# Multi-resolution attention with a mixture-of-experts stage: the loads are issued by GpSimd instead of ScalarE

## The chip, the cores and the metric

The program runs on one core of a Trainium2 chip. The metric is device time in microseconds of one execution, as the median of several runs. The engines are written as in the profile: PE (TensorE), DVE (VectorE), ACT (ScalarE), POOL (GpSimd) and SP (SyncE). Each of them takes its own instructions in one fixed order. A name with a q, as ACTq, is the engine's sequencer, which waits on semaphores and issues DMAs.

## The reference

For each of 8 batches, 8 heads, 576 tokens and a head dimension of 64, two attentions are added and then 128 tokens per batch go through a small feed-forward block:

```
q_d, k_d, v_d = means of q, k, v over groups of 4 tokens
out_up    = repeat(softmax(q_d k_d^T / 8) v_d, 4 times along the tokens)
out_local = softmax(q k^T / 8 where |i - j| < 4, else -1e9) v
x = (out_up + out_local) laid out as [batch, 576, 512]
scores = x . w_gate
for each batch: top = the 128 tokens of the highest score
    out[top] = x[top] + sigmoid(scores[top]) * (relu(x[top] @ w1) @ w2)
```

The feed-forward block is called MoE below.

## The kernel before

**Stages of one batch b.** `load_qk` brings q and k of a batch into the tile `T` in two DMAs (half the head pairs each, two runs of 4.6 KB per partition), `load_vw` brings windows of v into `vw` in three DMAs, and the first step of `pool_v` brings v in groups of four tokens into `vraw` in one DMA. `pool_qk` (VectorE) sums groups of four tokens of `T` into `dT`, and the rest of `pool_v` (GpSimd, lines 207 to 213) does the same for `vraw` into `vd` and `vr`, three sums and one product. `coarse` computes the coarse attention in two units; its second unit ends with the tile `ods` (L319), which SyncE stores to a DRAM buffer `up_d` with four copies of each row. `load_up` reads that back as `x` (SyncE). `local` computes the banded attention in three units of two, two and one tiles of 116 tokens; each tile ends with `t` on VectorE (L451). `sums` lets GpSimd add `x` and `t` (L469), five sums to a batch, and SyncE stores each group to the output. `route` ranks the tokens; VectorE writes the row numbers `idx` (L528), and GpSimd gathers the 128 rows back from the output into `xe` with an indirect DMA (L536). TensorE transposes them (`px`, L544), `moe` runs the two matrix products with the weights `w1` and `w2` (held as two f16 parts, made from the f32 staging tiles `stg` by ScalarE and VectorE in `load_weights`), and GpSimd scatters the rows back with a second indirect DMA (L587).

**Order of the work.** The stages are generators, and the table `PLACE` with the list `events` says at which point of the batch's period each step is traced. A load of batch b+1 is traced in the period of batch b: the `vraw` load at 0.217 of it, the three `vw` loads at 0.675, 0.925 and 1.175, the two `T` loads at -0.1 and 0.0 before the period in which they are pooled; the eight weight loads at 0.07 to 1.09 of the first period. `route` and `moe` of batch b run in the periods of b+1 and b+2. A planner then orders each engine's instructions by a simulated time line. What goes through the class `InOrder` (line 48 on, recorded in the profile under L55) is pinned: it is issued no earlier than the instruction that was traced just before it on the same engine. GpSimd's sums, products and indirect DMAs are not pinned and the planner may move them.

**What a DMA waits for.** The DMAs that ScalarE and SyncE issue share eight semaphores in turn. The next DMA on a semaphore is issued only once the one before on it has landed, whichever engine issued that.

**Buffers.** `T` and `vraw` have two buffers, `stg` four, `vw` one for each of its three parts.

**Lines.** `load_constants` 113 to 132, `load_weights` 142 to 165, `load_qk` 169 to 176, `load_vw` 192 to 198, `pool_v` 202 to 217, `sums` L466 to 478, `route` L481 to 552, `moe` from L555.

Of the kernel before, what the change touches and what calls it, by code (L numbers as in the profile page):

```python
# [21 lines left out]
P = 128  # L22
# [36 lines left out]
def tile_multires_attention_moe(ctx: ExitStack, tc: tile.TileContext, qk, vw, vp, cs, w_gate, w1, w2, outs):  # L59


    nc = tc.nc
    B, _, _, HP, S = qk.shape
    pool = nc.gpsimd
    sp, aq, vq = (InOrder(tc, e) for e in (nc.sync, nc.scalar, nc.vector))
    D = P // 2
    H = 2 * HP
    DM = H * D
# [22 lines left out]
    cst = cpool.tile([P, sum(CONST.values())], F32, name="cst")  # L91
    at = dict(zip(CONST, np.cumsum([0, *CONST.values()]).tolist()))

    def const(n):
        return cst[:, at[n] : at[n] + CONST[n]]

    wg = cpool.tile([P, DM], F32, name="wg")
# [15 lines left out]
    def load_constants():  # L113
        n = at["first"]
        sp.dma_start(out=cst[:, :n], in_=cs[:, :n])
        for t in (*qzbuf, *pzbuf, first):
            pool.memset(t, 0.0)
        pool.memset(ones, 1.0)
        nc.vector.tensor_copy(identb, ident)
        nc.vector.tensor_copy(mask.rearrange("p e t k -> p (e t k)"), const("mask"))  # L120
        for t in vals:
            nc.vector.tensor_copy(t[:, :, 0], const("tok"))
        nc.vector.tensor_copy(pen, const("pen"))
        nc.vector.tensor_copy(off, const("off"))
        yield
        aq.dma_start(out=wg, in_=w_gate.unsqueeze(0).broadcast_to([P, DM]))
        aq.dma_start(
            out=wgr, in_=w_gate.rearrange("(h d) -> h d", d=D).unsqueeze(1).broadcast_to([H, SR, D])
        )
        aq.dma_start(out=cst[:, n:], in_=cs[:, n:])  # L130
        pool.tensor_copy(first[:, :P], const("first"))
        yield

# [8 lines left out]
    def load_weights():  # L142
        pend = []

        def convert(sv, h_, l_):
            aq.activation(h_, sv, AF.Copy, scale=WS)
            vq.scalar_tensor_tensor(out=l_, in0=sv, scalar=WS, in1=h_, op0=ALU.mult, op1=ALU.subtract)

        for src, hi, lo, n in ((w1, w1h, w1l, DF), (w2, w2h, w2l, DM)):
            for i in range(4):  # L150
                cc = hi.shape[1] // 4
                stg = ld.tile([P, 4 * 256], F32, tag="stg", name="stg", bufs=4)
                sv = stg.rearrange("p (c f) -> p c f", f=n)
                aq.dma_start(
                    out=sv, in_=src[i * cc * P : (i + 1) * cc * P, :].rearrange("(c p) f -> p c f", p=P)
                )
                cs_ = slice(i * cc, (i + 1) * cc)
                pend.append((sv, hi[:, cs_, :], lo[:, cs_, :]))
                if len(pend) == 4:
                    convert(*pend.pop(0))  # L160
                yield
        while pend:
            convert(*pend.pop(0))
            yield
# [4 lines left out]
    def load_qk(b):  # L169
        qkT[b] = wk.tile([P, 2, HP, S], F32, tag="T", name=f"T{b}")  # L170
        hh = HP // 2
        for u in range(2):
            aq.dma_start(
                out=qkT[b][:, :, hh * u : hh * (u + 1)], in_=qk[b][:, :, hh * u : hh * (u + 1)]
            )
            yield
# [15 lines left out]
    def load_vw(b):  # L192
        vwin[b] = []
        for i, tiles in enumerate(TU):
            t = wk.tile([P, 2 * len(tiles), HP, D1], F32, tag=f"vw{i}", name=f"vw{b}_{i}", bufs=1)
            aq.dma_start(out=t, in_=vw[b][:, 2 * tiles[0] : 2 * tiles[-1] + 2])
            vwin[b].append(t)
            yield

# [1 line left out]

    def pool_v(b):
        raw = ld.tile([P, FACTOR, DM + D], F32, tag="vraw", name="vraw", bufs=2)
        aq.dma_start(out=raw, in_=vp[b])
        yield
        vd = vds[b] = wk.tile([P, DM + D], F32, tag="vd", name=f"vd{b}")
        pool.tensor_tensor(out=vd, in0=raw[:, 0], in1=raw[:, 1], op=ALU.add)  # L207
        for r in range(2, FACTOR):
            pool.tensor_tensor(out=vd, in0=vd, in1=raw[:, r], op=ALU.add)
        yield  # L210

        vrs[b] = wk.tile([P, H, D], F32, tag="vr", name=f"vr{b}", bufs=1)
        pool.tensor_tensor(
            out=vrs[b], in0=vd[:, DM:].unsqueeze(1).broadcast_to([P, H, D]),
            in1=bk.unsqueeze(2).broadcast_to([P, H, D]), op=ALU.mult,
        )
        yield
# [413 lines left out]
    nu = len(WU)  # L631
    mains = []
    consts = load_constants()
    next(consts)
    lqk = [put(lambda b=b: load_qk(b), 2, *when("QK", b, b - 1)) for b in range(B)]
    weights = None
    for b in range(B):
        pq = put(lambda b=b: pool_qk(b), 5, *when("PL", b, b - 1), lqk[b])
        pv = put(lambda b=b: pool_v(b), 3, *when("VP", b, b - 1))
        lv = put(lambda b=b: load_vw(b), 3, *when("VW", b, b - 1))  # L640
        if weights is None:
            put(lambda: consts, 1, *when("CS", 0, -1))
            weights = put(load_weights, 11, *when("WT", 0, 0))
        for i in range(nu):
            need = (pq, pv) if i < 2 else ()
            g = put(lambda b=b, i=i: unit(b, i), 0, 0, 0, *need)
            e0, e1 = ends[i], ends[i + 1]
            for ph in range(3):
                events.append((b + e0 + PH[ph] * (e1 - e0), len(events), g, ph == 2))
            mains.append(g)  # L650
        xl = put(lambda b=b: load_up(b), 1, *when("XL", b, b))
        xsums[b] = put(lambda b=b: sums(b), 3, *when("XS", b, b), xl)
        rt = put(lambda b=b: route(b, scs[b]), 15, *when("RT", b, b + 1), *mains[-nu:])
        put(lambda b=b: moes[b], 16, *when("MO", b, b + 1), weights, rt)
# [81 lines left out]
```

## Time and profile before

| | |
|---|---|
| median of 3 runs | 380.62 us (380.48 to 385.15) |
| profiled execution | 377.89 us, its span 376.1 us |
| busy PE / DVE / ACT / POOL | 287.4 / 248.9 / 143.8 / 127.4 us |
| share of the span | 76% / 66% / 38% / 34% |
| DMA moved | 78.25 MB, mean 208 GB/s |
| mean granted TensorE clock | 0.841 |

Times in the rows are microseconds from the start of the span. A row of the time line has the start, the length, the engine, the line of the code, the operation, the tile written, the tile read, and in brackets how long the engine had been idle and what ended that. A busy engine is one that executes; waiting and issuing by its sequencer is not counted, except for GpSimd's DMAs, which count as GpSimd's own work.

### The profile page before, as it was taken

How to read it: one execution, taken by the hardware profiler on the slowest of the kernel's cores; microseconds unless marked ns; L12 is line 12 of the kernel's file. 1: busy time of each engine (PE TensorE's matmuls, PEld its weight loads, DVE VectorE, ACT ScalarE, POOL GpSimd, SP SyncE). 2: the span in 40 equal slices, each digit the busy share in tenths (PEclk: the TensorE clock that was granted, in tenths of full speed). 3: DMA queues.
4: the chain of work that ended last, by engine and by line, in shares of the span. 5: the costliest groups of instructions: out<-in, count | busy, mean ns of one | idle time of the engine just before them, and what ended most of it. 6: DMA issues, size and time to landing. Idle time of an engine off the chain costs nothing.

```text
span 376.1 us, 10940 instructions
## 1 busy us (share of the span) xinstructions
PE 287.4 (76%) x4624; PEld 224.8 (60%) x4624; DVE 248.9 (66%) x534; ACT 143.8 (38%) x401; POOL 127.4 (34%) x99
## 2 busy tenths in 40 slices
PE   0680677717799999949996789919997799984984
PEld 0470546606687688638854677619865588673571
DVE  2595867995489777966776658855778667575030
ACT  0541357621445364513623264413624255424010
POOL 1505530471306630753045410733146410351111
PEclk9996556865699999957999599966999589998598
DMA  8897999782686969774777397765687343733100
GB/s 309 294 408 245 281 324 359 256 219 56 218 293 215 251 229 337 202 204 137 262 271 199 106 292 288 190 200 149 240 281 223 86 132 116 200 95 72 28 30 28
DMA packets 32832, 78.25 MB, mean 208 GB/s; under 512 B 7824, under 2 KB 7824, under 8 KB 31760
## 3 DMA queue, kind: packets, MB, share of 16 engines
q10 hardware_dynamic: 11048, 43.72, 33.5%
q1 hardware_dynamic: 20456, 29.65, 28.1%
q0 software_dynamic: 1280, 4.20, 3.5%
q8 instruction: 36, 0.59, 0.6%
q14 instruction: 12, 0.10, 0.1%
HBM read 56.58 MB, written 20.97 MB: 206 GB/s over the span
## 4 chain that ended last, share of the span: by engine, by line
PE 35%; DMA 30%; DVE 14%; issue 10%; ACT 7%; SPq 2%; POOL 1%; ACTq 1%; POOLq 0%; DVEq 0%
DMA up_d<-ods 11%; DMA x<-up_d 7%; DMA xe<-out_dram,idx 6%; ACT ed L262 4%; DMA out_dram<-xe,idx 3%; PE od L296 3%; PE ph L564 3%; PE ol L441 3%; PE ph L567 3%; PE sd L237 2%; PE ph L568 2%; PE pspl L429 2%; DMA T<-in_qk_dram 2%; SPq L55 2%; PE sl L407 2%
## 5 line engine op out<-in xcount | busy, mean ns | idle before, releaser
L469 POOL TENSOR_TENSOR x<-x,t 128x512 f32<-128x512 f32 x40 | 64.5, 1618 | 71.7 <-DVE t L451 55.4
L567 PE MATMUL ph<-xel,w1h 128*128 128x128 f16 x256 | 49.2, 230 | 1.6 <-DVE xel L548 1.6
L564 PE MATMUL ph<-xeh,w1h 128*128 128x128 f16 x256 | 49.7, 231 | 0.8 <-ACT xeh L547 0.7
L207 POOL TENSOR_TENSOR vd<-vraw 128x576 f32<-128x576 f32 x8 | 12.1, 1512 | 111.4 <-DMA vraw<-in_vp_dram 97.3
L568 PE MATMUL ph<-xeh,w1l 128*128 128x128 f16 x256 | 49.1, 230 | 0.0
L441 PE MATMUL ol<-vw,pt 64*64 64x65 f32 x1280 | 33.7, 255 | 19.9 <-DVE den L450 10.1
L55 DVE TENSOR_REDUCE dT<-T 128x288 f32<-128x1152 f32 x32 | 42.8, 1343 | 4.0 <-DMA T<-in_qk_dram 4.0
L441 PEld LDWEIGHTS ol<-vw,pt 64*64 64x64 f32 x1280 | 28.3, 163 | 25.3 <-ACT qz L189 10.4
L429 PE MATMUL pspl<-cst,ex 128*128 128x128 f32 x160 | 28.0, 315 | 11.5 <-ACT ex L423 11.5
L423 ACT ACTIVATE ex<-ex 128x1024 f32<-128x1024 f32 (+1 forms) x24 | 21.9, 913 | 33.3 <-DVE ex L419 17.5
L407 PE MATMUL sl<-T 64*58 64x64 f32 (+1 forms) x1280 | 33.6, 230 | 0.0
L456 DVE SCALAR_TENSOR_TENSOR jk<-t,wg 128x512 f32<-128x512 f32 x40 | 30.4, 763 | 1.0
L451 DVE TENSOR_TENSOR t<-ol,den 128x512 f32<-128x512 f32 x40 | 27.6, 692 | 4.0 <-DVE den L450 0.5
L407 PEld LDWEIGHTS sl<-T 64*58 64x58 f32 (+1 forms) x1280 | 28.2, 138 | 2.7 <-issue 0.8
L431 ACT COPY pt<-pspl 128x512 f32<-128x512 f32 x40 | 22.3, 582 | 19.1 <-PE pspl L429 18.9
L564 PEld LDWEIGHTS <-w1h 128*128 128x128 f16 x256 | 26.9, 105 | 3.1 <-issue 1.9
L429 PEld LDWEIGHTS pspl<-cst,ex 128*128 128x128 f32 x160 | 20.5, 161 | 13.7 <-ACT ex L423 12.0
L568 PEld LDWEIGHTS <-w1l 128*128 128x128 f16 x256 | 26.7, 104 | 2.2 <-issue 1.8
L567 PEld LDWEIGHTS <-w1h 128*128 128x128 f16 x256 | 26.8, 105 | 0.4
L262 ACT ACTIVATE ed<-sd,mxd 128x144 f32<-128x144 f32 x64 | 25.9, 524 | 0.5
L503 DVE SCALAR_TENSOR_TENSOR beat<-srow,scp,first 128x640 bf16<-128x640 f32 (+4 forms) x40 | 25.6, 673 | 0.0
L416 DVE TENSOR_REDUCE mx<-sl 128x16 f32<-128x1024 f32 (+1 forms) x24 | 24.8, 1033 | 1.1 <-PE sl L407 1.1
(132 smaller groups left out, 589.2 us busy)
## 6 DMA issues: line engine op xcount, KB each, us to landing
T<-in_qk_dram ACTq DMA_DIRECT2D x16, 1152.0 KB
vraw<-in_vp_dram ACTq DMA_DIRECT2D x8, 1152.0 KB
vw<-in_vw_dram ACTq DMA_DIRECT2D x16, 520.0 KB
up_d<-ods SPq DMA_DIRECT2D x8, 1024.0 KB
x<-up_d SPq DMA_DIRECT2D x32, 256.0 KB
out_dram<-x SPq DMA_DIRECT2D x32, 192.0 KB
stg<-in_moe_w_dram ACTq DMA_DIRECT2D x8, 512.0 KB
vw<-in_vw_dram ACTq DMA_DIRECT2D x8, 260.0 KB
```

Of the source, the lines that this page charges most:

```text
L55: return lambda *a, **k: self.tc.keep_in_program_order(f(*a, **k))
L262: nc.scalar.activation(ed[:, :, h] if h < H else er, s[:, a, SD * i : SD * (i + 1)], AF.Exp, bias=mx[:, c : c + 1], scale=pscale, accum_ou ...
L407: nc.tensor.matmul(s[64 * e : 64 * e + qn, a, c : c + KW], lhsT=T[64 * a : 64 * a + 64, 0, hp, q0s[blk] : q0s[blk] + qn], rhs=T[64 * a : 6 ...
L429: nc.tensor.transpose(ps[:, hp, :], ex[:, HP * i + hp, :], ident)
L441: nc.tensor.matmul(o[64 * e : 64 * e + 64, a, D1 * hp : D1 * (hp + 1)], lhsT=pt[64 * a : 64 * a + 64, hp, 64 * e : 64 * e + 64], rhs=vl[64 ...
L451: nc.vector.tensor_tensor(out=t.rearrange("p (g a d) -> p a g d", a=2, d=D), in0=ov[:, :, :, 0:D], in1=den.unsqueeze(3).broadcast_to([P, 2 ...
L456: nc.vector.scalar_tensor_tensor(out=jk, in0=t, scalar=1.0, in1=wg, op0=ALU.mult, op1=ALU.mult, accum_out=sc[:, j : j + 1],)
L469: pool.tensor_tensor(out=x[:, i], in0=x[:, i], in1=ts[b][j], op=ALU.add)
L503: nc.vector.scalar_tensor_tensor(out=beat[:, : NT - j].rearrange("p j u -> p (j u)"), in0=sr[:, P * j :], scalar=scp[:, j : j + 1], in1=fi ...
L564: nc.tensor.matmul(ph[:, i, :], lhsT=w1h[:, c, fs], rhs=xeh[:, c, :], start=c == 0, stop=False)
L567: nc.tensor.matmul(ph[:, i, :], lhsT=w1h[:, c, fs], rhs=xel[:, c, :], start=False, stop=False)
L568: nc.tensor.matmul(ph[:, i, :], lhsT=w1l[:, c, fs], rhs=xeh[:, c, :], start=False, stop=c == NC - 1)
```

## The change

All 59 loads from the inputs (three constants' loads, eight of weights, sixteen of `T`, twenty-four of `vw`, eight of `vraw`) are issued by GpSimd through `InOrder` instead of by ScalarE. The stores, the loads of `x` and the first load of constants stay with SyncE; the conversions of the weights stay pinned on ScalarE and VectorE.

```diff
-    sp, aq, vq = (InOrder(tc, e) for e in (nc.sync, nc.scalar, nc.vector))
+    sp, aq, vq, lq = (InOrder(tc, e) for e in (nc.sync, nc.scalar, nc.vector, nc.gpsimd))
...
-        aq.dma_start(out=wg, in_=w_gate.unsqueeze(0).broadcast_to([P, DM]))
-        aq.dma_start(
+        lq.dma_start(out=wg, in_=w_gate.unsqueeze(0).broadcast_to([P, DM]))
+        lq.dma_start(
             out=wgr, in_=w_gate.rearrange("(h d) -> h d", d=D).unsqueeze(1).broadcast_to([H, SR, D])
         )
-        aq.dma_start(out=cst[:, n:], in_=cs[:, n:])
+        lq.dma_start(out=cst[:, n:], in_=cs[:, n:])
         pool.tensor_copy(first[:, :P], const("first"))
...
                 sv = stg.rearrange("p (c f) -> p c f", f=n)
-                aq.dma_start(
+                lq.dma_start(
...
         for u in range(2):
-            aq.dma_start(
+            lq.dma_start(
                 out=qkT[b][:, :, hh * u : hh * (u + 1)], in_=qk[b][:, :, hh * u : hh * (u + 1)]
...
-            aq.dma_start(out=t, in_=vw[b][:, 2 * tiles[0] : 2 * tiles[-1] + 2])
+            lq.dma_start(out=t, in_=vw[b][:, 2 * tiles[0] : 2 * tiles[-1] + 2])
...
-        aq.dma_start(out=raw, in_=vp[b])
+        lq.dma_start(out=raw, in_=vp[b])
```

## Rows read from the trace of the kernel before

**Rows 1.** The page: busy time of the engines, and DMA share in 40 slices.
```profile
PE 287.4 (76%) x4624; PEld 224.8 (60%) x4624; DVE 248.9 (66%) x534; ACT 143.8 (38%) x401; POOL 127.4 (34%) x99
...
DMA  8897999782686969774777397765687343733100
```

**Rows 2.** Stretches: length, busy us (instructions) of each engine, clock, DMA share, GB/s.
```profile
24.00:67.00 43.00, 25.31 (x439) 20.23 (x427) 31.97 (x59) 18.44 (x45) 13.66 (x9) 0.64 0.95 317
...
148.00:190.00 42.00, 35.40 (x561) 28.08 (x551) 29.78 (x65) 17.03 (x49) 15.80 (x11) 0.84 0.72 220
```

**Rows 3.** The page: the chain that ended last, shares by engine.
```profile
PE 35%; DMA 30%; DVE 14%; issue 10%; ACT 7%; SPq 2%; POOL 1%; ACTq 1%; POOLq 0%; DVEq 0%
```

**Rows 4.** Time line of PE, 0 to 112 us: start, length, work, idle before.
```profile
36.93 1.97 PE L429 MATMUL pspl<-cst,ex 128*128 128x128 f32 x8 [8.49 <-ACT ex L423]
...
48.99 1.12 PE L429 MATMUL pspl<-cst,ex 128*128 128x128 f32 x4 [2.99 <-ACT ex L423]
...
86.41 1.09 PE L544 MATMUL px<-cst,xe 128*128 128x128 f32 x4 [10.14 <-DMA xe<-out_dram,idx]
```

**Rows 5.** Time line of ACT and its queue, 0 to 190 us.
```profile
0.74 1.32 ACTq L55 DMA_DIRECT2D T<-in_qk_dram  x2
...
14.68 0.57 ACTq L55 DMA_DIRECT2D T<-in_qk_dram  x1
...
20.51 0.39 ACTq L55 DMA_DIRECT2D vraw<-in_vp_dram  x1
...
35.44 0.34 ACTq L55 DMA_DIRECT2D stg<-in_moe_w_dram  x1
35.82 1.06 ACT L423 ACTIVATE ex<-ex 128x1024 f32<-128x1024 f32 x1 [9.33 <-DMA up_d<-ods]
...
47.36 1.06 ACT L55 ACTIVATE w1h<-stg 128x1024 f16<-128x1024 f32 x1 [5.94 <-DMA x<-up_d]
...
62.90 0.37 ACTq L55 DMA_DIRECT2D vraw<-in_vp_dram  x1
...
158.14 0.34 ACTq L55 DMA_DIRECT2D vw<-in_vw_dram  x1
```

**Rows 6.** Time line of POOL, the whole span.
```profile
2.10 0.09 POOL L118 MEMSET ones<- 128x1 bf16 x1
12.67 1.40 POOL L207 TENSOR_TENSOR vd<-vraw 128x576 f32<-128x576 f32 x1 [10.48 <-DMA vraw<-in_vp_dram]
...
17.23 1.04 POOL L213 TENSOR_TENSOR vr<-vd,cst 128x512 f32<-128x512 f32 x1
31.77 1.88 POOL L207 TENSOR_TENSOR vd<-vraw 128x576 f32<-128x576 f32 x1 [13.50 <-DMA vraw<-in_vp_dram]
...
42.21 6.34 POOL L469 TENSOR_TENSOR x<-x,t 128x512 f32<-128x512 f32 x4 [4.49 <-DMA x<-up_d]
...
70.87 1.40 POOL L207 TENSOR_TENSOR vd<-vraw 128x576 f32<-128x576 f32 x1 [15.77 <-DMA vraw<-in_vp_dram]
...
77.45 1.95 POOL L536 DMA_INDIRECT xe<-out_dram,idx  x1 [0.17 <-DMA x<-up_d]
...
159.43 2.95 POOL L469 TENSOR_TENSOR x<-x,t 128x512 f32<-128x512 f32 x2 [1.64 <-DMA x<-up_d]
162.53 0.98 POOL L536 DMA_INDIRECT xe<-out_dram,idx  x1 [0.15 <-issue]
```

**Rows 7.** Time line of DVE, 0 to 112 us.
```profile
74.81 0.15 DVE L528 CAST idx<-pi 128x1 int32<-128x1 f32 x1
```

**Rows 8.** Groups of POOL: count, then busy us, mean ns, idle before, and releasers.
```profile
L536 POOL DMA_INDIRECT xe<-out_dram,idx x8 | 9.1, 1136 | 35.5 <-DVE den L449 19.4 <-DVE idx L528 12.0 <-DMA out_dram<-x 3.5
...
L587 POOL DMA_INDIRECT out_dram<-xe,idx x8 | 8.1, 1006 | 24.2 <-DVE xe L586 24.1 <-issue 0.2
```

**Rows 9.** The page: DMA issues, count and KB each.
```profile
T<-in_qk_dram ACTq DMA_DIRECT2D x16, 1152.0 KB
...
vw<-in_vw_dram ACTq DMA_DIRECT2D x16, 520.0 KB
```

## The prediction

> **What bounds the kernel now.** I read the page first: PE is busy 76% of the span, DVE 66%, ACT only 38% and POOL 34%, and the DMA engines are nearly full in the first seven slices and less so after [rows 1]. So a mean tells nothing, and I cut the span into stretches. From 24 to 67 us, DMA is the full resource (0.95 busy, 317 GB/s) while PE works 25 of 43 us at a clock of 0.64; from 148 to 190, one period of the steady part, PE works 35 of 42 us and DMA is at 0.72 [rows 2]. The start is a matter of transfers and their order, the steady part of PE and of what PE waits for. The chain that ended last says the same: PE 35%, DMA 30%, and the issuing queue that the change empties, ACTq, 1% [rows 3].
>
> Then I asked what PE waits for. Two waits early on, 8.49 and 2.99 us, end with ACT, and one of 10.14 us, at 86.41, ends with the landing of the first gather [rows 4]. ACT itself was held in the first case: its `ex` at 35.82 came 9.33 us late, after the landing of an `up_d` store, because a weight load stood ahead of it in the queue and waited for a semaphore that the store of SyncE still held; the conversion at 47.36 came 5.94 us late behind a load of `x` in the same way [rows 5]. These two stalls are what the change takes away for certain.
>
> The gather at 77.45 is the other thing to see [rows 6]. Its row numbers were there at 74.96 [rows 7], but in POOL's queue it stands behind the four operations of `vd` and `vr`, which started at 70.87 when `vraw` had landed after 15.77 us of idling [rows 6]. That `vraw` load was issued at 62.90 [rows 5]. So the first long wait of PE hangs, over POOL's fixed order, on the moment when the third `vraw` load is issued. The same order holds the gather at 162.53 behind the two sums at 159.43, which had waited for `x` [rows 6].
>
> **The change part by part.** *What goes from ACTq.* All 59 issues, and with them the two stalls. Of the chain, 1% of 376.1 us, 3.8 us, is ACTq [rows 3]; the first load's 0.66 us (half of 1.32) is in it and comes back on POOL [rows 5], so I credit 3.1 us (bounds 0 and 5.6, as the 1% is rounded and another wait may stand behind it). The two PE waits, 11.5 us together, I do not credit: PE next stands at the wait for the gather, and ACT being earlier does not move that. They are the gain of a rival below.
>
> *What POOL pays for one issue.* No row shows a plain load issued by POOL. The nearest is its own indirect DMA with 128 rows: 1.14 and 1.01 us as means [rows 8], 1.95 at the longest [rows 6]; from below, ACTq's 0.34 to 0.66 us [rows 5]. I take 1.0 us for a load with one run per partition, as the indirect DMA is made by the same engine with as many rows, and 1.5 for the 20 loads with two runs (`T` and the weights of `w2`), between one price and two. That is 39 + 30 = 69 us more for POOL, 196 of 376, and 7 us a period on top of the 15.8 of 42 that it is busy [rows 2]. As work this hides in its idle time. What does not hide is where the loads stand in its order.
>
> *The first loads.* They are pinned behind the last memset, which ends at 2.19 instead of the 0.74 at which ACTq began: 1.45 us later [rows 5, 6]. Two `T` loads of 1152 KB [rows 9] and a `vraw` load as large by its shape, 3.54 MB, take 11.2 us at 317 GB/s, so with one issue ahead the first `vraw` is there at about 14.5 instead of 12.67 [rows 2, 6].
>
> *The hole behind them.* The program traces the first sums of `vd` ahead of the constants' loads, so these three are now pinned behind sums that wait for `vraw`. From 14.5 to the end of the sums, 4.6 us later, nothing new is asked for, in the stretch where DMA is the full resource. Sums to 19.1, three loads to 22.1, `vr` of 1.04 to 23.1: only now, instead of at 14.68, comes the first `T` load of the second batch. With it, two `vw`, the other `T`, a weight load, a `vw` and the small copy (7.3 us together), the second `vraw` is issued at 30.4 instead of 20.51. It landed 11.3 us after its issue before [rows 5, 6]; the same again gives 41.7, and the four POOL operations, 5.6 us as at 12.67 to 18.27, end at 47.3.
>
> *The second round.* Next in the order come a weight load (1.0), the four sums of `x` (6.34 [rows 6]), and then four weight loads, three `vw`, two `T` and the fifth sum (6 + 3 + 3 + 1.6): the third `vraw` is issued at 68.2 instead of 62.90 [rows 5], 5.3 us late. `vd`, the gather and `px` follow it one for one, since PE idles there with nothing else ahead: **+5.3 us**. Bounds: 0, if the earlier end of ACT's stalls lets the sums and conversions start sooner; +18 more, if each of the 19 issues between the hole and this point takes 1.95 instead.
>
> *The steady part.* Each period's first `vw` load is pinned behind the second sum of `x`. Where the gather comes right after that sum, the load can stand between: its 1.0 us, and the 0.53 MB [rows 9] that then run ahead of the gather's rows, 1.7 us at 317 GB/s. Of the seven periods, the gather at 162.53 is the one where this is plain [rows 6]; ACTq issued that load at 158.14 [rows 5]. I count one: **+2.7 us** (bounds 0 and seven of them, 18.9). The other loads are asked for on POOL at nearly the time that ACT now asks for them, because both stand behind work of the same units; nothing that they wait for (a buffer that PE has read) is later than what the sum ahead of them waited for. Their cover is POOL's idling before `vd`; if that were gone, each microsecond of issue would push the gathers.
>
> *Sum.* 5.3 + 2.7 - 3.1 = 4.9. The profiled execution took 377.89 us around its span of 376.1, and is 2.7 below the median of the runs, 380.62; 377.89 + 4.9 + 2.7 = **385.5 us**, its own range 378 to 393.
>
> **The rivals.** *The freed ACT queue wins.* If the order on POOL lets the first gather pass ahead of `vd`, that gather needs only `idx`, and the chain to `idx` runs through PE and ACT, which lose the waits of 8.49 and 2.99 us [rows 4]. Price: 11.5 less the 1.45 of the later first load, 10 us: 370.6. For it: `idx` stood ready 2.5 us before the gather [rows 6, 7], and the planner may move the gather, which is not pinned. Against it: a DMA stretch at 0.95 [rows 2] with a hole added.
>
> *POOL's one queue holds the gathers.* Loads that stand ahead of the gather in every period, at 2.7 us each in seven periods, are 18.9; with the start and the credit, 5.3 - 3.1, that is 21: 401.7. It decides where the second sum of `x` ends before the gather's row numbers and stores are there. For it: at 162.53 it was so [rows 6], and one indirect DMA took 1.95 us against a mean of 1.14 [rows 6, 8], so an issue can nearly double. Against it: POOL idles 66% of the span [rows 1]. The Trainium skill, in "SBUF — State Buffer", section "Who interferes with whom", has a rule against such a move: GpSimd's descriptor writing is shut out while VectorE runs in a mode that takes both shared ports, and a load from another queue is not. By that rule issues would stretch as this one did; no row here shows the mode.
>
> *Only the issuing moves.* The full resource of the start is the DMA engines [rows 2], and the bytes stay the same. If the loads land as before, what remains is 1.45 late at the start and 3.1 saved: 379. The Trainium skill, in "DMA: Bandwidth & Descriptors", section "Issuing engines are not separate DMA queues", says just this: the queues share the same engines, and another issuer saves only issue time. The 9.33 us that a queue stood still for another queue's semaphore [rows 5] speaks against taking it as all there is.
>
> **How the numbers follow.** Chances: the forecast 0.42, the freed ACT queue 0.20, the held gathers 0.25, only the issuing 0.13. Two per cent of 380.62 is 7.6, about what a measurement here can tell from no change: within lies 373.0 to 388.2. Of the forecast, 0.29 lies within and 0.13 above; of the freed queue, 0.18 below and 0.02 within. So faster 0.18, same 0.29 + 0.02 + 0.13 = 0.44, slower 0.13 + 0.25 = 0.38. The range goes from just under the freed queue's price to that of the held gathers, **369 to 402**.
>
> **What would show it.** ACT without the waits of 9.33 and 5.94 us, whatever the time. POOL's first `vd` near 14.5, the constants' loads behind it, DMA slices near 15 to 20 us emptier, the second batch's first `T` load near 23, the third `vraw` load near 68, `px` of the first batch 5 us late. Loads of one run at about 1.0 us on POOL. The forecast is wrong if the gather stands ahead of `vd`, if issues are under 0.5 or near 2 us, if the loads' longer way makes `dT` late (VectorE waiting for `T` for more than a few us), or if the planner, given other issue costs, orders PE and VectorE anew.

## The result, and the profile after

The changed kernel takes **382.8 us** (median of 12 runs) against 377.91 us for the kernel before (12 runs of the same chips): a ratio of **1.0149, 95% interval 1.0117 to 1.0181**, 4.9 us more, within the 2% of "no change" and by its interval slower. Its profiled execution took 383.54 us around a span of 381.8, 5.7 us more than the 376.1 of before. (A ratio leaves out the runs that lie more than 1.5% above the fastest of their kernel, here also one run of the changed kernel of 624.37 us that stays unexplained, and the kernel before spreads over 372 to 390 us from run to run; so medians are given beside ratios below.)

The page first: busy time, DMA slices (each 9.5 us) and the chain by engine, of the changed kernel.

```profile
PE 289.1 (76%) x4624; PEld 224.9 (59%) x4624; DVE 254.6 (67%) x534; ACT 143.3 (38%) x401; POOL 164.6 (43%) x158
...
DMA  6389868966387859866936868466957624821000
...
PE 35%; DVE 19%; DMA 19%; issue 10%; ACT 8%; POOL 5%; SPq 2%; POOLq 0%; DVEq 0%
```

POOL is busy 37 us longer than in [rows 1], for 59 more instructions, and ACTq has left the chain of [rows 3]. The second DMA slice has fallen from 8 to 3: the hole that was forecast. The same in stretches, of the changed kernel: length, busy us (instructions) of PE, PEld, DVE, ACT and POOL, granted clock, DMA share, GB/s.

```profile
0.00:24.00 24.00, 10.00 (x122) 7.64 (x123) 11.16 (x18) 7.44 (x28) 13.54 (x25) 1.00 0.57 193
24.00:67.00 43.00, 18.53 (x336) 14.34 (x334) 26.14 (x46) 12.44 (x26) 23.18 (x26) 0.61 0.87 297
...
78.00:317.00 239.00, 204.97 (x3393) 162.35 (x3392) 183.48 (x389) 101.62 (x295) 114.61 (x98) 0.87 0.68 214
```

From 24 to 67 us PE works 18.5 us instead of 25.3 [rows 2]. The last row, from the second batch's `ods` to the last one's, has its counterpart before, from 67 to 316 us:

```profile
67.00:316.00 249.00, 203.96 (x3425) 162.93 (x3425) 179.91 (x393) 102.73 (x295) 93.42 (x65) 0.85 0.67 208
```

The same PE work fits into 10 us less. So time was lost at the start and won back in the middle. To size this I cut each span at three events that every kernel has: the second batch's `ods` on VectorE (L319), the last batch's `ods`, and the issue of the last scatter (L587). What lies behind that issue is the close. All in us, from the time lines:

```
                  to ods(1)  ods(1)-ods(7)  of it ods(4)-ods(6)  to last scatter  close   span
before              67.1        248.5            85.6              56.0           4.6    376.1
after               77.8        239.1            79.4              56.8           8.0    381.8
start_on_act        70.5        248.4            81.3              56.4           6.1    381.4
steady_on_act       77.3        245.0            86.9              59.5           5.2    387.0
first_on_dve        69.2        249.0            79.0              57.5           8.0    383.6
extra59             68.9        258.3            89.6              55.1           8.0    390.4
extra59_1row        68.9        255.9            90.0              55.0           8.0    387.8
weights_on_pool     68.0        248.3            88.5              55.9           4.6    376.8
before_idxs         70.9        245.2            85.9              55.9           4.5    376.5
before_xe3          69.8        245.4            85.4              54.1           4.7    373.9
before_idxs_xe3     70.2        241.3            80.9              54.6           4.7    370.8
xe3_five            68.5        245.0            81.3              54.2           4.7    372.4
after_idxs_xe3      76.8        235.6            78.4              57.1           8.0    377.4
consts_on_act       67.6        237.1            78.3              56.8           7.7    369.2
```

The change: **+10.8** at the start, **-9.3** in the middle, +0.8, **+3.4** at the close; together 5.7. How much of this is chance can be read in the table too: before, before_idxs, before_xe3, before_idxs_xe3 and xe3_five have the same order on every engine, and their first column runs from 67.1 to 70.9, their second from 241.3 to 248.5; the last two of them are one and the same program, and differ by 3.7 us there. So 3 to 4 us in one of these is no finding; the third column, 85.4 to 85.9 in the first three, 80.9 and 81.3 in the other two, is steadier.

*The start.* POOL's time line of the changed kernel, with what stood there before in [rows 6] and, for the loads, on ACTq in [rows 5]:

```profile
2.14 1.65 POOL L55 DMA_DIRECT2D T<-in_qk_dram  x2
...
14.10 1.40 POOL L207 TENSOR_TENSOR vd<-vraw 128x576 f32<-128x576 f32 x1 [9.76 <-DMA vraw<-in_vp_dram]
...
18.41 0.59 POOL L55 DMA_DIRECT2D wg<-in_moe_w_gate_dram  x1
...
21.21 0.77 POOL L55 DMA_DIRECT2D T<-in_qk_dram  x1
...
25.88 0.30 POOL L131 COPY first<-cst 128x128 f32<-128x128 f32 x1
29.16 0.53 POOL L55 DMA_DIRECT2D vw<-in_vw_dram  x1 [2.98 <-DMA T<-in_qk_dram]
...
66.91 0.55 POOL L55 DMA_DIRECT2D vraw<-in_vp_dram  x1
81.46 1.41 POOL L207 TENSOR_TENSOR vd<-vraw 128x576 f32<-128x576 f32 x1 [14.01 <-DMA vraw<-in_vp_dram]
...
89.62 3.47 POOL L469 TENSOR_TENSOR x<-x,t 128x512 f32<-128x512 f32 x2 [1.22 <-DMA x<-up_d]
93.05 0.58 POOL L55 DMA_DIRECT2D vw<-in_vw_dram  x1
93.93 1.05 POOL L536 DMA_INDIRECT xe<-out_dram,idx  x1 [0.31 <-issue]
```

The constants' loads stand behind the first sums, as forecast; behind them the copy into `first`; and behind that the first batch's first `vw` load, which also waited 2.98 us until a `T` load had landed, and went at 29.16 us. Before, ACTq issued it at 4.97. PE shows who needed it; first the same load and the first `ol` of the kernel before, then PE's waits in the changed kernel:

```profile
4.97 0.52 ACTq L55 DMA_DIRECT2D vw<-in_vw_dram  x1
26.06 0.70 PE L441 MATMUL ol<-vw,pt 64*64 64x65 f32 x32
```

```profile
44.55 2.01 PE L441 MATMUL ol<-vw,pt 64*64 64x65 f32 x64 [6.12 <-DMA vw<-in_vw_dram]
...
99.70 1.08 PE L544 MATMUL px<-cst,xe 128*128 128x128 f32 x4 [8.33 <-DMA xe<-out_dram,idx]
```

The first `ol` starts at 44.6 us (26.1 before), and the wait for the first gather's rows ends at 99.70 instead of 86.41 [rows 4]. ACT's two stalls of [rows 5] are gone; the operation that waited 9.33 us now has no wait:

```profile
35.37 1.04 ACT L423 ACTIVATE ex<-ex 128x1024 f32<-128x1024 f32 x1
```

*The middle.* Before, PE's longest wait after that for the first gather is one of 7.19 us. Time lines of PE, DVE and POOL of the kernel before, around 250 us:

```profile
241.56 1.01 POOL L587 DMA_INDIRECT out_dram<-xe,idx  x1 [0.15 <-issue]
...
249.84 0.99 POOL L536 DMA_INDIRECT xe<-out_dram,idx  x1 [3.48 <-DMA out_dram<-x]
...
249.14 0.16 DVE L528 CAST idx<-pi 128x1 int32<-128x1 f32 x1 [4.42 <-DMA out_dram<-xe,idx]
...
252.70 1.15 PE L441 MATMUL ol<-vw,pt 64*64 64x65 f32 x32 [7.19 <-DVE den L450]
```

Batches are counted from 0, as in the code. VectorE's `idx` of batch 4 stood until the scatter of the batch before it had landed, and VectorE's `den`, for which PE waited, stood behind it. Of the changed kernel the same row numbers and the same gather:

```profile
251.89 0.16 DVE L528 CAST idx<-pi 128x1 int32<-128x1 f32 x1 [0.72 <-PE pi L524]
252.70 1.27 POOL L536 DMA_INDIRECT xe<-out_dram,idx  x1 [0.16 <-DMA x<-up_d]
```

No scatter is waited for, and the gather goes 0.7 us after its row numbers, in a kernel that was 8.8 us late at batch 4's `ods`. The code of `idx` and `xe` is the same in both kernels and asks for three and two buffers. What differs is where the builder of the program, which orders the instructions and places the tiles in memory, put them: in the built program of the kernel before, `idx` of batches 2, 3 and 4 has one address, and `xe` of these batches too; in that of the changed kernel both take two addresses in turn. Why the builder did so was not looked into.

*The close.* The last instruction of weight is a DRAIN on POOL's queue at L730, here for before and after: durations in ns, least, median, longest of three.

```profile
L730 POOLq DRAIN  x3: 40/102/3678, 371.3 to 375.5; - x3
```

```profile
L730 POOLq DRAIN  x3: 46/97/7430, 373.5 to 381.5; - x3
```

It is 3.75 us longer, and the program ends with it.

### The profile page after: what moved, and what is told of

It reads as the page before. It is cut to its first block, busy times and chain, and to the rows that moved or that the text cites. A ratio compares the mean times of both kernels' runs of the same rounds, so it can differ in the third digit from the quotient of the medians.

```text
span 381.8 us, 10933 instructions
## 1 busy us (share of the span) xinstructions
PE 289.1 (76%) x4624; PEld 224.9 (59%) x4624; DVE 254.6 (67%) x534; ACT 143.3 (38%) x401; POOL 164.6 (43%) x158
## 2 busy tenths in 40 slices
DMA packets 31576, 78.25 MB, mean 205 GB/s; under 512 B 7712, under 2 KB 7712, under 8 KB 30504
## 4 chain that ended last, share of the span: by engine, by line
PE 35%; DVE 19%; DMA 19%; issue 10%; ACT 8%; POOL 5%; SPq 2%; POOLq 0%; DVEq 0%
DMA xe<-out_dram,idx 4%; DMA vw<-in_vw_dram 4%; ACT ed L262 4%; PE ol L441 3%; DMA up_d<-ods 3%; PE od L296 3%; PE pspl L429 3%; DMA vraw<-in_vp_dram 3%; DVE dT L55 3%; PE sd L237 3%; PE ph L564 2%; PE ph L568 2%; PE ph L567 2%; DMA x<-up_d 2%; SPq L55 2%
## 5 line engine op out<-in xcount | busy, mean ns | idle before, releaser
L469 POOL TENSOR_TENSOR x<-x,t 128x512 f32<-128x512 f32 x40 | 65.3, 1637 | 72.4 <-DVE t L451 39.2
L441 PE MATMUL ol<-vw,pt 64*64 64x65 f32 x1280 | 35.3, 258 | 22.1 <-DVE den L450 6.4
L564 PE MATMUL ph<-xeh,w1h 128*128 128x128 f16 x256 | 48.7, 228 | 1.8 <-ACT xeh L547 1.8
L568 PE MATMUL ph<-xeh,w1l 128*128 128x128 f16 x256 | 48.3, 227 | 0.0
L441 PEld LDWEIGHTS ol<-vw,pt 64*64 64x64 f32 x1280 | 29.1, 166 | 29.2 <-issue 14.5
L407 PE MATMUL sl<-T 64*58 64x64 f32 (+1 forms) x1280 | 34.7, 234 | 0.0
L429 PE MATMUL pspl<-cst,ex 128*128 128x128 f32 x160 | 29.0, 321 | 5.5 <-ACT ex L423 5.1
L407 PEld LDWEIGHTS sl<-T 64*58 64x58 f32 (+1 forms) x1280 | 29.1, 141 | 3.0 <-issue 1.1
L503 DVE SCALAR_TENSOR_TENSOR beat<-srow,scp,first 128x640 bf16<-128x640 f32 (+4 forms) x40 | 28.9, 756 | 0.0
L237 PE MATMUL sd<-dT 64*128 64x144 f32 x128 | 18.7, 411 | 9.7 <-DVE dT L55 9.3
## 6 DMA issues: line engine op xcount, KB each, us to landing
vraw<-in_vp_dram POOLq DMA_DIRECT2D x8, 1152.0 KB, 12.4
```

What stands on the lines that cost most here:

```text
L237: nc.tensor.matmul(s[:, a, SD * i : SD * (i + 1)], lhsT=dT[64 * a : 64 * a + 64, 0, hp, :P], rhs=dT[64 * a : 64 * a + 64, 1, hp, :], start ...
L407: nc.tensor.matmul(s[64 * e : 64 * e + qn, a, c : c + KW], lhsT=T[64 * a : 64 * a + 64, 0, hp, q0s[blk] : q0s[blk] + qn], rhs=T[64 * a : 6 ...
L429: nc.tensor.transpose(ps[:, hp, :], ex[:, HP * i + hp, :], ident)
L441: nc.tensor.matmul(o[64 * e : 64 * e + 64, a, D1 * hp : D1 * (hp + 1)], lhsT=pt[64 * a : 64 * a + 64, hp, 64 * e : 64 * e + 64], rhs=vl[64 ...
L469: pool.tensor_tensor(out=x[:, i], in0=x[:, i], in1=ts[b][j], op=ALU.add)
L503: nc.vector.scalar_tensor_tensor(out=beat[:, : NT - j].rearrange("p j u -> p (j u)"), in0=sr[:, P * j :], scalar=scp[:, j : j + 1], in1=fi ...
```

## The experiments

First theory: the start is lost by loads that stand in POOL's order; the middle is won by loads that ACT no longer holds; the close grows with POOL's DMAs. Rival for the middle: the planner, given other costs, orders the engines anew.

**start_on_act** and **steady_on_act**: the change for one half of the loads each.

```diff
-            lq.dma_start(out=raw, in_=vp[b])          # so too for T and vw
+            (aq if b < 2 else lq).dma_start(...)      # start_on_act; constants and weights on aq too
+            (lq if b < 2 else aq).dma_start(...)      # steady_on_act
```

> The constants, the weights and the loads of batches 0 and 1 are issued by ScalarE again, those of batches 2 to 7 by GpSimd. Theory: the change loses about 10.7 us in the first two batches (ods of batch 1 at 77.8 instead of 67.1 us), wins about 9 us between ods of batch 1 and of batch 7 (239.2 us instead of 248.5), and pays 3.7 us at the end, where GpSimd's closing DRAIN takes 7.4 instead of 3.7 us in step with the DMAs that GpSimd issued. Then here ods of batch 1 comes at 67 to 68 us, the stretch to ods of batch 7 takes 239 to 241, the drain (52 instead of 75 GpSimd DMAs) about 6.0, and the span is about 371 to 373 us, 1 to 1.5% faster than before. Rival: the gain of the middle part is only the other order that the planner happened to write for TensorE and VectorE; then the stretch comes out anywhere from 239 to 250 and the span at 371 to 381.

> The opposite half: constants, weights and the loads of batches 0 and 1 by GpSimd, those of batches 2 to 7 by ScalarE. Theory: the start is lost as in the change, ods of batch 1 at 77 to 78 us, the middle is as before, 247 to 249 us to ods of batch 7, the drain with 39 GpSimd DMAs about 5.1 us; span 386 to 389 us, 2.5 to 3% slower than before. Rival (planner's orders decide the middle): the stretch between 239 and 250 with no tie to the issuer, span 378 to 389.

Measured: start_on_act 1.0056 (0.9985 to 1.0127), median 381.91 against 380.50; steady_on_act 1.0383 (1.0287 to 1.0479), 392.84. The second has the whole loss of the start (77.3) and little of the gain, as the theory said. The first keeps the start of before nearly (70.5), yet its middle is 248.4, not 239 to 241, and the fastest of its ten runs takes 376.67 us, where the theory wanted a span of 371 to 373: that part of the theory fell, as the rival had it. Moving the steady loads to POOL doesn't by itself make the middle short. Its third column (81.3) has the gain; but from `ods(3)` to `ods(4)` it takes 48.0 us against 42.3 in the changed kernel, at a mean granted clock of 0.79 against 0.84.

**first_on_dve**: the change, with the copy into `first` on VectorE, so that the first `vw` load no longer stands behind it.

```diff
-        pool.tensor_copy(first[:, :P], const("first"))
+        nc.vector.tensor_copy(first[:, :P], const("first"))
```

> As the change, but the small copy into first runs on VectorE, so that the first vw load is no longer pinned behind it and is issued near 20.2 instead of 29.2 us. Theory: TensorE's wait of 6.1 us at 44.55 for that load is gone, ol of batch 0 starts near 32 to 36 us instead of 44.6, and ods of batch 1 comes 4 to 8 us earlier than 77.8, the span 377 to 380. Rival: the late T loads (21.2 instead of 14.7 us) and VectorE's wait for them are what holds the start; then ol is earlier but ods of batch 1 stays at 76 to 79 us and the span at 380 to 383.

Measured: 1.0173 (1.0095 to 1.0251), 385.62. That `vw` load is now issued at 20.15, the first `ol` starts at 32.6, and `ods(1)` is back at 69.2. POOL's time line:

```profile
20.15 0.57 POOL L55 DMA_DIRECT2D vw<-in_vw_dram  x1
...
61.70 0.55 POOL L55 DMA_DIRECT2D vraw<-in_vp_dram  x1
76.61 1.71 POOL L207 TENSOR_TENSOR vd<-vraw 128x576 f32<-128x576 f32 x1 [14.36 <-DMA vraw<-in_vp_dram]
...
88.38 1.03 POOL L536 DMA_INDIRECT xe<-out_dram,idx  x1 [0.30 <-issue]
```

So the held `vw` load was what made `ods(1)` late. The time didn't follow, and the expected span of 377 to 380 was missed: the middle is 249.0 again. The loss lies between `ods(1)` and `ods(3)`, 88.7 us against 78.8 in the changed kernel; behind `ods(3)` the two agree (160.2 and 160.4). In these two periods PE is busy 6.9 us longer, at a mean granted clock of 0.68 and 0.92 instead of 0.76 and 1.00, and the planner gave it another order: to turn the changed kernel's order into this one, 362 of the 4200 matmuls and weight loads in PE's program have to be moved (312 for start_on_act). Whether the order or the clock costs the 10 us, and whether the one makes the other, is not settled.

**extra59** and **extra59_1row**: the kernel before, with 59 tiny loads on POOL behind the sums of `x`, of 128 rows of 8 bytes and of one.

```diff
+            for k in [k for _, k in zip(range(3), extra)]:
+                tc.keep_in_program_order(pool.dma_start(out=scratch[:P, k], in_=cs[:P, 2 * k : 2 * k + 2]))   # [:1, k], cs[:1] in extra59_1row
```

> The kernel before, all loads on ScalarE, with 59 additional DMAs of 8 bytes by 128 partitions issued by GpSimd after the sums of x, into a tile that nothing reads. Theory: the closing DRAIN of GpSimd grows with the number of DMAs that it issued: 75 instead of 16, as in the change, so about 7.4 instead of 3.7 us, although 59 DMAs carry 60 KB and not 43.7 MB. Rival: the drain grows with what GpSimd's queue moved, or with the rows it described last; then it stays at 3.7 to 4.5 us. The DMAs themselves take 0.5 to 0.6 us each of GpSimd, three at a time between sums; span 378 to 384 us by the theory.

> The kernel before with 59 more GpSimd DMAs of one row of 8 bytes each (in extra59 each had 128 rows). If the closing drain goes by the count of DMAs that GpSimd issued, it is 7.2-7.5 us again; if it goes by their rows, 3.7-4.6 us.

Measured: extra59 1.0125 (1.0006 to 1.0245), 389.06, longer than the expected span of 378 to 384; extra59_1row 389.56 in one run. The drain of extra59_1row:

```profile
L734 POOLq DRAIN  x3: 46/103/7417, 379.6 to 387.5; - x3
```

7.42 us in both, with next to no bytes and with one row each. (Their middle is longer too, 258.3 and 255.9 us; what of that is the loads' place and what a new order was not separated.) With the other kernels: 3.68 us at 16 POOL DMAs, 4.02 at 24, 4.62 at 39, 5.55 at 52, 7.18 at 72, 7.43 at 75. It goes by their count, though not in proportion: 23 more cost 0.94 us from 16 on and 1.88 from 52 on.

**weights_on_pool**: before, with only the eight weight loads on POOL.

```diff
-                aq.dma_start(        # stg
+                lq.dma_start(
```

> The kernel before with only the eight weight loads issued by GpSimd. Theory (the freed ScalarE): ScalarE's waits of 9.33 and 5.94 us behind its own loads go; batch 1's `ods` comes at 62-66 instead of 67.1 us, PE's waits of 8.49 and 2.99 us shrink to under 4 together, the closing drain is 4.0-4.6 us with 24 DMAs, and the time is 0.985-0.998 of before. Rival (GpSimd's order): the weight loads stand ahead of sums and of the first gather on GpSimd, that gather comes later than 77.5 by 3-8 us, and the time is 1.00-1.02.

Measured: 1.0112 (0.998 to 1.0244), median 377.81 against 378.79: no change that can be told. The first gather went 4.5 us later, at 82.0, as the rival had it, and the drain is 4.02 us, as the theory had it; but the test of the freed ScalarE is not clean, as ACT's stalls moved to the next loads in its queue. ACT's waits for DMAs, in total us, times, longest:

```profile
ACT qz L189 <- DMA up_d<-ods: 5.7, 1, 5.7
ACT ex L423 <- DMA vw<-in_vw_dram: 3.7, 1, 3.7
```

`ods(1)` came at 68.0, not at 62 to 66, and the first `px` at 86.6 (86.4 before). It does show that ACT's stalls and the issue of the first gather can both move by several us without moving the first `px`: the gather's rows came 4.6 us after its issue here, 9.0 before.

**before_idxs, before_idxs_xe3, before_xe3**: the wait at 250 us. `idx` and `xe` share places over the batches, as the built program has them; a new tile waits for the scatter that last read its place. These give each batch its own `idx`, or `xe` three tiles, or both; every engine's order stays that of before.

```diff
+    idxs = cpool.tile([P, 8], I32, name="idx"); xes = [cpool.tile([P, DM], F32, name=f"xe{i}") for i in range(3)]
...
-        idx = sm.tile([P, 1], I32, tag="idx", name="idx", bufs=3)
+        idx = idxs[:, b : b + 1]
...
-        xe = wk.tile([P, DM], F32, tag="xe", name="xe", bufs=2)
+        xe = xes[b % 3]
```

> The kernel before, with a column of its own for each batch's row numbers `idx` instead of buffers that are used again; the order on every engine stays the same. Theory: what the changed kernel wins back in its middle is this wait: VectorE's `idx` at 249.14 us stood 4.42 us for the landing of an earlier scatter, and PE stood 7.19 us at 252.70 behind VectorE's next `den`. Without it the PE wait there falls to under 4 us, the period from batch 5's `ods` to batch 6's from 43.7 to 39-41 us, and the time is 0.985-0.993 of before. Rival: the gather of that batch still waits for the same scatter, PE then waits for the gather's rows, and the period stays at 42-44, the time at 0.995-1.003.

> As before_idxs, and the gathered rows `xe` in three tiles taken in turn, so that the gather of batch 4 waits for the scatter of batch 1 and no longer for that of batch 3. Theory of the buffers: this gather moves from 249.8 us to 245-247, and the time is 0.983-0.992 of before, up to 2 us less than before_idxs. Rival: the gather's rows were not what PE stood for, and the two kernels are within 0.3% of each other.

> The kernel before with three `xe` tiles, but `idx` in shared buffers as before. Theory: `idx` of batch 4 still waits for the scatter of batch 3 and is there at 248-250 us, so the gather goes at 249-251 and the span is within 0.7% of 376.1; it takes both edits. Rival: the shared `xe` buffer alone was the wait, the gather goes at 244-247 and the span is 369-373.

> The kernel of before_idxs_xe3 again, with more rounds, because its time is to be settled: the kernel before with own row numbers and three `xe` tiles. Theory of the buffers: 0.980-0.990 of before, last scatter at 364-368. Rival: a lucky draw, 0.993-1.003.

Measured: before_idxs 1.0107 (1.0044 to 1.017), medians 377.1 against 378.79, which point the other way: no change that can be told. Its time lines of POOL and PE:

```profile
251.18 1.31 POOL L536 DMA_INDIRECT xe<-out_dram,idx  x1 [2.80 <-DMA out_dram<-x]
...
248.30 1.15 PE L441 MATMUL ol<-vw,pt 64*64 64x65 f32 x32 [2.74 <-DVE den L450]
255.09 1.09 PE L544 MATMUL px<-cst,xe 128*128 128x128 f32 x4 [5.64 <-DMA xe<-out_dram,idx]
```

`idx` comes at 244.68 instead of 249.14 and PE's wait of 7.19 shrinks to 2.74; but the gather goes no earlier, and PE waits at `px` instead. The row puts the gather's wait down to a store of `x`, the event that came last by the profile; that it was the buffer of `xe`, shared with the scatter at 241.81, is shown by the kernel that takes it away. before_xe3, one run of 375.65 us: the gather at 248.9, held by `idx`. Each alone leaves ods(4)-ods(6) at 85.4 to 85.9. Both together:

```profile
246.59 0.99 POOL L536 DMA_INDIRECT xe<-out_dram,idx  x1 [0.15 <-DVE dT L55]
...
248.12 1.15 PE L441 MATMUL ol<-vw,pt 64*64 64x65 f32 x32 [2.32 <-DVE den L450]
250.98 1.09 PE L544 MATMUL px<-cst,xe 128*128 128x128 f32 x4 [1.72 <-DMA xe<-out_dram,idx]
```

This is xe3_five: **0.990 (0.9851 to 0.995)**, median 373.44 against 377.06; before_idxs_xe3, the same kernel with fewer rounds, 373.32 against 378.79. ods(4)-ods(6) falls by 4.3 us (4.7 in before_idxs_xe3): the two waits stand in parallel, and only taking both away pays.

The other kernels say the same without these edits. Where the built program has one address for batches 2, 3 and 4 (before, steady_on_act, weights_on_pool, extra59, extra59_1row), `idx` of batch 4 waits 4.4 to 5.5 us for a scatter, and the third column is 85.6 to 90.0; where it has two in turn (after, start_on_act, first_on_dve, consts_on_act), there is no such wait, and the column is 78.3 to 81.3. Of steady_on_act and of start_on_act:

```profile
255.63 0.16 DVE L528 CAST idx<-pi 128x1 int32<-128x1 f32 x1 [4.73 <-DMA out_dram<-xe,idx]
```

```profile
250.76 0.10 DVE L528 CAST idx<-pi 128x1 int32<-128x1 f32 x1
```

The two addresses go with loads of batches 2 to 7 on POOL in all nine. So what the change won in ods(4)-ods(6) is the builder's placing of two tiles, not anything that an engine does faster.

**after_idxs_xe3**: the same two edits on the changed kernel.

> The changed kernel with the same two edits (own row numbers, three `xe` tiles). Theory: its gather of batch 4 waits for no scatter any more, so the edits give it nothing there, and its time stays at 1.010-1.018 of before, within 0.5% of the changed kernel; against the kernel before with these edits the change then costs 9-12 us instead of 5. Rival: the buffers cost the changed kernel as much as the kernel before, and it falls to 0.995-1.005.

Measured: 1.0187 (1.0124 to 1.025), median 382.96; the changed kernel alone has 382.8. The edits that save the kernel before 3.6 us give the changed one nothing in the time: it had won this already, with its two addresses. With them on both sides, the change costs 382.96 - 373.44 = 9.5 us instead of 4.9.

**consts_on_act**: the change, with the three loads of constants left on ScalarE.

```diff
-        lq.dma_start(out=wg, in_=w_gate.unsqueeze(0).broadcast_to([P, DM]))    # so too for wgr, cst
+        aq.dma_start(out=wg, in_=w_gate.unsqueeze(0).broadcast_to([P, DM]))
```

> The changed kernel, with the three loads of constants left on ScalarE. This closes the hole of the start: the copy into `first` and the first `vw` load then stand ahead of the first `vd` on GpSimd, and the second batch's first `T` load follows `vr` directly. Theory (the hole and the held `vw` load make the late start): batch 0's `ods` at 23-25 instead of 30.2, its first `ol` at 26-30 instead of 44.6, `ods` of batch 1 at 68-71 instead of 77.8, the first gather at 84-89 instead of 93.9 because `vd` of batch 2 still stands ahead of it; the drain 7.2-7.4; the time 1.000-1.010 of before. Rival (the queue as such: loads on GpSimd land late, whatever stands between them): `ods` of batch 1 at 75-78, the time 1.012-1.018.

Measured: **0.9947 (0.9903 to 0.9991)**, median 373.8 against 377.06: 9.0 us below the changed kernel's median, by its interval just faster than the kernel before though within the 2% of "no change", and faster than the theory's 1.000 to 1.010. POOL's time line:

```profile
7.85 0.29 POOL L131 COPY first<-cst 128x128 f32<-128x128 f32 x1 [3.51 <-DMA cst<-in_const_dram]
8.33 0.54 POOL L55 DMA_DIRECT2D vw<-in_vw_dram  x1 [0.20 <-issue]
15.34 1.39 POOL L207 TENSOR_TENSOR vd<-vraw 128x576 f32<-128x576 f32 x1 [6.46 <-DMA vraw<-in_vp_dram]
...
20.77 0.77 POOL L55 DMA_DIRECT2D T<-in_qk_dram  x1
...
59.12 0.55 POOL L55 DMA_DIRECT2D vraw<-in_vp_dram  x1
75.19 1.58 POOL L207 TENSOR_TENSOR vd<-vraw 128x576 f32<-128x576 f32 x1 [15.52 <-DMA vraw<-in_vp_dram]
...
85.78 1.03 POOL L536 DMA_INDIRECT xe<-out_dram,idx  x1 [0.30 <-issue]
```

The first `vw` load goes at 8.33 instead of 29.16, and `ods(1)` comes at 67.6 instead of 77.8. But the hole itself is still there: the second batch's first `T` load goes at 20.77 (21.21 in the changed kernel), as it still stands behind `vd` and `vr`. So most of the start's loss was not in the hole but in the one load of `vw`, held behind the copy that stood behind the constants; first_on_dve, which frees the same load in another way, says the same of `ods(1)`. Batch 0 stays late: its `ods` came at 28.05, not at 23 to 25 (30.16 in the changed kernel), its first `ol` at 30.7, not at 26 to 30. PE's order is near the changed kernel's (91 of 4200 to be moved), and the middle (237.1) and the close (7.7) stay. Its lead over the kernel before is the buffers' again: xe3_five, with all loads on ACT and buffers of its own, has the same time, 373.44.

## Why the prediction was right, and where only its total was

The time came out at 382.8 against a forecast of 385.5, and the difference at 4.9 us, the very number of the sum (4.9); the 2.7 us between the two times is what the three runs of before stood above the median of the twelve. The terms did not come out: +5.3, +2.7 and -3.1 stand against a measured +10.8, -9.3, +0.8 and +3.4. The start was under-sized, the close and the middle were left out, and these errors of opposite sign, each about as large as the sum or larger, cancelled. That the total agrees is luck: with `idx` and `xe` in buffers of their own on both sides, the change costs 9.5 us. Two of the signs that the prediction had set against itself did show: PE's order is new (333 of 4200 to be moved), and VectorE waited 4.76 us for the second batch's `T`, whose first sum came at 28.89 instead of 21.87.

- **The start, +5.3: right in mechanism, mis-sized.** The order was as forecast: `vd` at 14.10 (forecast 14.5), constants behind it, the second batch's `T` load at 21.21 (23), the third `vraw` load at 66.91 (68.2, 62.90 before). But "`vd`, the gather and `px` follow it one for one" failed three times. From its issue to its sum the load took 14.6 us instead of 8.0, so `vd` came 10.6 late. The gather then stood behind two sums of `x` and a `vw` load as well, 5.9 us more: 16.5 late. And its row numbers were themselves 13.5 late, at 88.34 instead of 74.81 [rows 7], 6 to 9 us of it through the held `vw` load (82.09 in first_on_dve and 79.07 in consts_on_act, which set it free). I had counted that load as an issue among others, and not asked who waits for it. `px` came 13.3 late, not 5.3. (The bound of +18 was also worked out too wide: eight of its 19 issues had been priced at 1.5 already, so 1.95 for each adds 14.)
- **What POOL pays for an issue: too high.** 37 us in all against the 69 taken. Of the changed kernel, POOL's loads: ns of least, median and longest.

```profile
L55 POOL DMA_DIRECT2D vw<-in_vw_dram x24: 531/561/578, 22.0 to 304.7; - x24
...
L55 POOL DMA_DIRECT2D T<-in_qk_dram x16: 701/721/901, 2.1 to 264.7; - x16
L55 POOL DMA_DIRECT2D vraw<-in_vp_dram x8: 531/540/561, 3.8 to 268.1; - x8
```

  The bound from below, ACTq's 0.34 to 0.66 us, was the nearer one. The 24 `vw` issues lie within 47 ns of each other: no sign here of POOL being shut out by VectorE, which is busy 67%, as the Trainium skill's "SBUF — State Buffer", section "Who interferes with whom", would allow for.
- **The gathers behind a load, +2.7: not seen.** A `vw` load ahead of a gather costs its 0.6 us, and the period in which the gather at 162.53 lay, from batch 3's `ods` to batch 4's, is 42.3 us against 42.5. The rival of the held gathers (401.7) fell with it: POOL's gathers idled 13.4 us instead of 35.5 [rows 8].

```profile
L536 POOL DMA_INDIRECT xe<-out_dram,idx x8 | 8.9, 1112 | 13.4 <-DVE idx L528 10.6 <-DMA x<-up_d 2.1 <-issue 0.6
```

- **ACT's stalls, credited with nothing: not refuted.** They went, and nothing in the start came earlier. The 3.1 us for ACTq's share of the chain can't be told apart in any of these differences. The rival of the freed queue (370.6) was wrong in its reason: the gather stayed behind `vd`. A time near its own was within reach, as consts_on_act shows with 373.8, but through the buffers.
- **The middle, costed at nothing: wrong by some 9 us.** I had read the 35 of 42 us in one period and not the period with the 7.19 us wait, whose reason, a shared buffer and a scatter, stands in the trace of before; that the builder would place the buffers otherwise could not be read there. Of the 9.3, 6.2 lie in ods(4)-ods(6), and own buffers in the unchanged order give 4.3 to 4.7 of them. The other 3.1 are less than what two profiles of one program differ by there (3.7), and what makes them isn't settled: PE's order is another (the planner, which I had named as a risk), and the granted clock of the middle is 0.87 instead of 0.85.
- **The close, not in the sum: +3.4.** No row of before could show its dependence; the DRAIN's own 3.68 us could have been asked about.
- **Only the issuing moves (379): refuted.** The Trainium skill's "DMA: Bandwidth & Descriptors", section "Issuing engines are not separate DMA queues", says that another issuer saves only issue time. The bytes are the same here (78.25 MB in both), but the cost is more than that: between the changed kernel and consts_on_act only three loads of together some 0.56 MB change their issuer, and the median changes by 9.0 us.

## What to carry to other kernels

When loads move to another in-order queue, look for the smallest of them that something waits for, and for what it now stands behind: one `vw` load behind one copy behind three constants made `ods(1)` some 9 us late, while the 37 us of the 59 issues hid in POOL's idle time. Take two waits that end together (`idx` and `xe` on one scatter) away together, or not at all, and look up where the builder put the tiles: the code asked for three and two buffers, and three batches in a row shared one. And when a forecast total comes out right, check its terms at fixed events before believing the sum.

## What the runs showed of the hardware

- POOL's closing DRAIN grows with the number of DMAs that POOL issued, from 3.68 us at 16 to 7.43 at 75, and not with their bytes or rows (7.42 for 75 of which 59 moved 8 bytes each).
- A plain load costs POOL 0.53 to 0.90 us to issue here (medians 0.54 to 0.72 by tile), less than its gather (1.11 in the mean).
- With the `vraw` loads on POOL they took 12.4 us in the median to land; the third took 14.6, 14.9 and 16.1 us to its sum (the changed kernel, first_on_dve, consts_on_act), where ACTq's took 8.0. It is so in the steady part too: the last five took 5.2 to 6.7 us from issue to sum on ACTq (before, steady_on_act) and, but for one of each kernel (7.2 and 6.2), 11.1 to 13.6 on POOL (after, start_on_act). Whether the queue or the loads issued with it made that was not taken apart.
